# Float16 pairs for the scores of every second group of four heads, and six weight groups converted beside the attention

## The chip, the cores and the metric

One core of a Trainium2 chip. The time is the device time of one execution in microseconds. Engines: TensorE (PE, with its weight loads as PEld), VectorE (DVE), ScalarE (ACT), GpSimd (POOL) and SyncE (SP), whose queue issues nearly all transfers.

## The reference

Sigmoid attention, then a gated layer on its output, with q, k and v in float32 and the weights in float64:

```python
scores = scale * np.matmul(q, k.transpose(0, 1, 3, 2)) - np.log(S)   # 8 batches, 12 heads, S = 448, head size 64
attn = 1.0 / (1.0 + np.exp(-scores))
attn_out = np.matmul(attn, v)
x = attn_out.transpose(0, 2, 1, 3).reshape(B * S, H * D)             # 3584 x 768
gate = 1.0 / (1.0 + np.exp(-(x @ w_gate)))                           # w_gate, w_val: 768 x 1536
val = x @ w_val
out = gate * val @ w_out                                             # w_out: 1536 x 768
```

## The kernel before

It runs in two stages. The first is the attention, with the conversion of some weights beside it; the second the gated layer, in visits: four pairs of batches, each visited for two parts of the hidden size ("A"), then the output ("C"). Its products are in float16 pairs: a float32 value is scaled by a power of two and split into a high half (a cast) and a low half (value times scale minus the high half), and three products (high by high, high by low, low by high) go into one accumulator. They are formed by seven products in place of eight (N_OPS = 7 operands per block).

**The attention.** A group m is four heads of one batch, two pairs p of two heads h; there are 24. `load_qk` and `load_v` bring q, k and v of a group. A beat (m, g), g from 0 to 6, is one call of `scores` and, LAG = 2 beats behind it, one of `values`. `scores` fills a PSUM tile `sc` by four float32 products of 64x64 array tiles (L502; each is two instructions in the trace), so that four run side by side, and ScalarE makes `a` of it with one sigmoid over 896 columns (L510). `values` multiplies by v into accumulators `av` (L527). Two accumulators per pair hold the two halves of the keys; `finish` copies one by ScalarE (L537), and VectorE adds the other (L544). The result goes to DRAM and is read back as x.

Two PSUM tiles `sc` exist, and three `a`; every engine works through its instructions in the order written.

**The weights** come as 64-bit floats. `Words` loads a block of 128x384 (a chunk; `AHEAD` of them are loaded ahead) and turns it into float32 by integer operations: the magnitude of the upper words (L214) by VectorE, a limit by GpSimd (L195), then in `first` two VectorE instructions (L201, L202), in `second` three (L209 to L211), and a maximum (L107). `convert` does this in steps, two to a chunk: an even step holds `first` and the next chunk's magnitude, an odd one the limit and `second`. Eight steps make a group (one of the twelve halves of jp, `halves_of_jps`). Six steps later its scale is known: the largest value of each row, clamped (L116), is spread over the partitions by TensorE (`told`, L508, which writes beside the scores in `sc`) and ScalarE (L513), and VectorE makes powers of two of it (L126, L120 to L123). Then seven operands are cast by GpSimd (L377, with sums by L259 for four of them), two steps later VectorE makes the low halves (L229), and SP stores them. In the step the low halves come first, then the maximum, then the chunk's own work, then what falls due of a scale.

FIRST groups are converted in the attention, the others of part 0 in the first visit, all others later. `BESIDE` says how many steps are done by which beat (`done`, in the loop over beats). After the steps, the beat does the work on x of the first pair: loads with maxima, sums, and splits (L385 is the low half) from certain m on.

**The order of a beat** is scores, values, loads, stores, weight steps, adds, x. In the visits a tick is one product group of nine instructions (L659); `beside` runs the weight steps due at each tick, and `Visit.tick` the loads, sums and splits of the next x. `load_operands` keeps RING + BEYOND = 11 operands loaded or known ahead.

Of the kernel before, what the change touches and what calls it, by code (L numbers as in the profile page):

```python
# [20 lines left out]
P = 128  # L21
# [9 lines left out]
BESIDE = 146, 168  # L31

AHEAD, AHEAD_FF = 4, 3

FIRST = 7
# [20 lines left out]
def sigmoid_attention_glu_kernel(ctx: ExitStack, tc: tile.TileContext, qk, v, wg, wv, wo, out):  # L56
# [111 lines left out]
    class Words:  # L168
# [28 lines left out]
        def first(self):  # L197

            raw, f = self.begun[0]
            e = f.bitcast(U32)  # L200
            nc.vector.tensor_scalar(out=e, in0=e, scalar1=3, scalar2=0x3F800000, op0=ALU.logical_shift_left, op1=ALU.bitwise_and)  # L201
            nc.vector.scalar_tensor_tensor(out=e, in0=raw[:, :, 1], scalar=0xC0000000, in1=e, op0=ALU.bitwise_and, op1=ALU.bitwise_or)  # L202

        def second(self):

            raw, f = self.begun.pop(0)
            self.spent += 1
            m = self.pool.tile([P, CW], U32, tag="wm", name="wm", bufs=1)
            nc.vector.tensor_scalar(out=m, in0=raw[:, :, 1], scalar1=11, scalar2=0x80000000, op0=ALU.logical_shift_left, op1=ALU.bitwise_or)  # L209
            nc.vector.scalar_tensor_tensor(out=m, in0=raw[:, :, 0], scalar=21, in1=m, op0=ALU.logical_shift_right, op1=ALU.bitwise_or)  # L210
            nc.vector.scalar_tensor_tensor(out=f, in0=m, scalar=2.0 ** -31, in1=f, op0=ALU.mult, op1=ALU.mult)  # L211
# [266 lines left out]
    with tc.manual_schedule(), tc.tile_pool(name="att", bufs=2) as att, tc.tile_pool(name="sc", bufs=2, space=PSUM) as scp, \  # L478
            tc.tile_pool(name="av", bufs=1, space=PSUM) as avp:
        loads, avs, pending, adds, stores = {}, {}, [], [], []  # L480

        def load_qk(m):

            if m < B * NQ:
                loads[m] = [att.tile([P, 2, 2 * S], F32, tag="qk", name="qk")]
                nc.sync.dma_start(out=loads[m][0], in_=qk[m // NQ, m % NQ])

        def load_v(m):
            if m < B * NQ:
                loads[m].append(att.tile([P, 7, 2, D], F32, tag="v", name="v"))  # L490
                nc.sync.dma_start(out=loads[m][1], in_=v[m // NQ, m % NQ])

        def scores(m, g):


            qkt = loads[m][0]
            sc = scp.tile([P, 2, 512], F32, tag="sc", name="sc")
            for h in range(2):
                for u in range(2):
                    p = u if g == 3 else g // 4  # L500
                    k0 = S + (3 * P if g == 3 else g % 4 * P + u * HP)
                    nc.tensor.matmul(sc[halves[u], h, :S], lhsT=qkt[halves[h], p, k0:k0 + HP], rhs=qkt[halves[h], p, :S],  # L502
                                     start=True, stop=True)
            told = spreads[:1]
            for sp in told:
                spreads.remove(sp)
                for h in range(2):
                    nc.tensor.matmul(sc[:, h, S:], lhsT=sp.each, rhs=ident[:, halves[h]], start=True, stop=True)  # L508
            a = att.tile([P, 2, S], F32, tag="a", name="a", bufs=3)
            nc.scalar.activation(a, sc[:, :, :S], AF.Sigmoid, bias=bias, scale=scale)  # L510
# [5 lines left out]
        def values(m, g, a):  # L516

            vt = loads[m][1]
            for u in range(2):
                p = u if g == 3 else g // 4  # L520
                key = (2 * m + p, u)
                start = key not in avs
                if start:
                    avs[key] = avp.tile([P, 512], F32, tag=f"av{p}{u}", name="av")
                last = (3 if u == 0 else 2) if p == 0 else 6
                for h in range(2):
                    nc.tensor.matmul(avs[key][halves[h], :S], lhsT=vt[halves[u], g, h], rhs=a[halves[u], h],  # L527
                                     start=start, stop=g == last)
            if g == 3:
                finish(2 * m)  # L530
            if g == 6:
                finish(2 * m + 1)

        def finish(n):
            b, c = divmod(n, 2 * NQ)
            x = att.tile([P, S], F32, tag="x", name="x", bufs=3)
            nc.scalar.copy(x, avs.pop((n, 0))[:, :S])  # L537
            adds.append((beat, x, avs.pop((n, 1))[:, :S]))
            stores.append((beat + 3, b, c, x))

        def finish_adds(wait=0):
            while adds and adds[0][0] + wait < beat + (not wait):
                _, x, other = adds.pop(0)
                nc.vector.tensor_tensor(out=x, in0=other, in1=x, op=ALU.add)  # L544
# [38 lines left out]
        beat = 0  # L583
        for m in range(B * NQ):
            for g in range(7):
                pending.append((m, g, scores(m, g)))
                if len(pending) > LAG:
                    values(*pending.pop(0))
                if g == 0:
                    load_qk(m + 1)  # L590
# [4 lines left out]
                while done < n_chunks and done * BESIDE[0] < beat * n_chunks or \  # L595
# [469 lines left out]
```

## Time and profile before

| | |
|---|---|
| median of 3 runs (lowest, highest) | 1126.88 us (1126.84, 1127.08) |
| the profiled execution's own time | 1127.14 us |
| its span | 1125.4 us |
| TensorE, VectorE, ScalarE, GpSimd busy | 99%, 70%, 60%, 44% |
| attention | up to 261.98 us |
| granted clock of TensorE | 0.999 |

A row of the timeline is: start in us, length in us, engine, line, operation, tile written and read, count, and in brackets the idle time before it and what ended it. A row of groups has count, busy us, mean ns, and idle time. Mean times of TensorE's products are pipelined, and four tiles overlap: 537 ns is not what one costs.

### The profile page before, as it was taken

What the parts mean: (1) busy time and instruction counts of PE and PEld (TensorE: products, weight loads), DVE (VectorE), ACT (ScalarE), POOL (GpSimd) and SP (SyncE); (2) the same over time, 40 slices, a digit from 0 to 9 for tenths busy, and PEclk for the clock granted to TensorE, in tenths of its full rate; (3) what the DMA queues carried; (4) which work ended last, traced back from release to release, by engine and by line L of the source; (5) the groups of instructions that cost most, each with busy time, mean ns of one, the idle gap of its engine ahead of it and who ended that gap; (6) DMA issues with size and microseconds to landing.
All of it is one profiled execution on the core that took longest, in us unless ns stands there. A gap on an engine that the chain in (4) does not pass through costs nothing.

```text
span 1125.4 us, 20712 instructions
## 1 busy us (share of the span) xinstructions
PE 1119.5 (99%) x7269; PEld 554.4 (49%) x7269; DVE 790.4 (70%) x1318; ACT 672.2 (60%) x1265; POOL 496.9 (44%) x424
## 2 busy tenths in 40 slices
PE   9999999999999999999999999999999999999998
PEld 4444434445555555555555555555555555555554
DVE  3578989974574555667678887887348687676863
ACT  6777778876775765766565756666444444253430
POOL 0045778791252332253233443333365294572940
PEclk9999999999999999999999999999999999999999
DMA  7679979888687746753566798979756876867644
GB/s 254 233 245 326 320 251 316 302 281 303 241 274 254 254 144 213 265 163 104 151 216 207 236 355 256 322 235 256 223 167 200 252 225 206 277 199 247 190 127 140
DMA packets 174536, 265.30 MB, mean 236 GB/s; under 512 B 49248, under 2 KB 151392, under 8 KB 174432
## 3 DMA queue, kind: packets, MB, share of 16 engines
q1 hardware_dynamic: 174144, 263.80, 72.6%
q8 instruction: 57, 0.93, 0.3%
q14 instruction: 47, 0.39, 0.1%
q10 hardware_dynamic: 288, 0.18, 0.1%
HBM read 182.48 MB, written 81.43 MB: 235 GB/s over the span
## 4 chain that ended last, share of the span: by engine, by line
PE 99%; ACT 0%; DVE 0%; DVEq 0%; issue 0%
PE un L659 76%; PE av L527 11%; PE sc L502 11%; PE sc L565 0%; PE sc L508 0%; ACT a L510 0%; PE un L627 0%; DVE g L944 0%; DVEq L1060 0%; DVE bias L79 0%; DVEq L944 0%
## 5 line engine op out<-in xcount | busy, mean ns | idle before, releaser
L659 PEld LDWEIGHTS <-A 128*128 128x128 f16 x3024 | 295.5, 98 | 275.8 <-issue 0.7
L659 PE MATMUL un<-b,A 128*128 128x448 f16 x1512 | 296.6, 352 | 0.0
L659 PE MATMUL un<-b,v 128*128 128x448 f16 x1512 | 296.3, 352 | 0.0
L659 PE MATMUL un<-hh,A 128*128 128x448 f16 x1008 | 273.0, 352 | 0.0
L659 PEld LDWEIGHTS <-v 128*128 128x128 f16 x1512 | 147.8, 98 | 137.7
L510 ACT ACTIVATE a<-sc,bias 128x896 f32<-128x896 f32 x168 | 169.5, 1010 | 62.4 <-PE sc L502 54.5
L659 PE MATMUL un<-hl,A 128*128 128x448 f16 x504 | 177.6, 352 | 0.0
L527 PE MATMUL av<-a,v 64*64 64x448 f32 x1344 | 166.5, 537 | 0.0
L502 PE MATMUL sc<-qk 64*64 64x448 f32 x1344 | 165.8, 537 | 0.4 <-ACT a L510 0.4
L869 POOL TENSOR_TENSOR g<-c,g 128x448 f32<-128x448 f32 x44 | 59.1, 1344 | 184.9 <-DVE c L642 98.2
L195 POOL TENSOR_SCALAR wf<-wf 128x384 f32<-128x384 f32 x72 | 41.9, 582 | 204.3 <-ACT wf L217 131.8
L854 ACT ACTIVATE g<-c,back 128x448 f32<-128x448 f32 x72 | 48.2, 670 | 77.6 <-DVE c L642 75.1
L502 PEld LDWEIGHTS sc<-qk 64*64 64x64 f32 x1344 | 56.1, 133 | 74.7 <-issue 59.5
L642 DVE TENSOR_TENSOR c<-un,u 128x448 f32<-128x448 f32 x72 | 44.8, 622 | 66.6 <-PE un L659 58.3
L527 PEld LDWEIGHTS av<-a,v 64*64 64x64 f32 x1344 | 56.0, 133 | 68.9 <-issue 64.8
L259 POOL TENSOR_TENSOR wf<-wf 128x384 f32<-128x384 f32 x72 | 82.7, 1154 | 13.2 <-DVE whl L229 12.2
L345 POOL TENSOR_TENSOR v<-v 128x448 f32<-128x448 f32 x48 | 64.0, 1362 | 51.6 <-DVE hl L385 50.6
L345 POOL TENSOR_TENSOR b<-b 128x448 f32<-128x448 f32 x48 | 67.5, 1442 | 40.6 <-DVE hl L385 40.6
L675 ACT COPY p<-un 128x448 f32<-128x448 f32 x48 | 25.6, 533 | 57.9 <-PE un L659 57.6
L345 POOL TENSOR_TENSOR r<-r 128x448 f32<-128x448 f32 x36 | 46.5, 1306 | 24.2 <-DVE b L385 23.8
L544 DVE TENSOR_TENSOR x<-av,x 128x448 f32<-128x448 f32 x48 | 29.8, 620 | 38.8 <-ACT x L537 37.6
L104 ACT ACTIVATE junk<-g 128x448 bf16<-128x448 f32 x88 | 50.7, 576 | 7.4 <-POOL g L869 5.9
(348 smaller groups left out, 1361.2 us busy)
## 6 DMA issues: line engine op xcount, KB each, us to landing
A<-ad SPq DMA_DIRECT2D x168, 192.0 KB, 3.3
A<-oo SPq DMA_DIRECT2D x168, 192.0 KB, 2.6
qk<-qk SPq DMA_DIRECT2D x23, 896.0 KB, 5.5
h<-g SPq DMA_DIRECT2D x88, 224.0 KB, 3.4
ad<-whl SPq DMA_DIRECT2D x84, 192.0 KB, 4.1
bd<-b SPq DMA_DIRECT2D x30, 448.0 KB, 3.5
b<-bd SPq DMA_DIRECT2D x30, 448.0 KB, 5.8
v<-vv SPq DMA_DIRECT2D x24, 448.0 KB, 5.1
```

The lines of the kernel that those rows point to most:

```text
L104: nc.scalar.activation(junk[:, :x.shape[-1]], x, AF.Abs, accum_out=to)
L195: nc.gpsimd.tensor_scalar(out=f, in0=f, scalar1=F32_MAX, scalar2=F64_ZERO, op0=ALU.min, op1=ALU.max)
L259: nc.gpsimd.tensor_tensor(out=x, in0=y, in1=z, op=op)
L345: engine.tensor_tensor(out=to, in0=x, in1=y, op=ALU.subtract)
L502: nc.tensor.matmul(sc[halves[u], h, :S], lhsT=qkt[halves[h], p, k0:k0 + HP], rhs=qkt[halves[h], p, :S], start=True, stop=True)
L510: nc.scalar.activation(a, sc[:, :, :S], AF.Sigmoid, bias=bias, scale=scale)
L527: nc.tensor.matmul(avs[key][halves[h], :S], lhsT=vt[halves[u], g, h], rhs=a[halves[u], h], start=start, stop=g == last)
L544: nc.vector.tensor_tensor(out=x, in0=other, in1=x, op=ALU.add)
L642: engine.tensor_tensor(out=to, in0=x, in1=y, op=ALU.add)
L659: nc.tensor.matmul(acc, lhsT=w, rhs=m, start=begin and i == 0, stop=i == len(terms) - 1, skip_group_check=not begin)
L854: nc.scalar.activation(gates[i], acc, AF.Sigmoid, scale=of_unit[0])
L869: nc.gpsimd.tensor_tensor(out=h, in0=acc, in1=gates[i], op=ALU.mult)
```

## The change

- Groups with odd m (`in_halves`) have their scores in float16 pairs: `split_qk` makes, beside group m - 1, the largest magnitudes of q and k (one reduction), their clamped values `told`, and, from the sums `total` over the partitions (TensorE products with `ones`, a ScalarE copy), powers of two; then high and low halves `hl` of q and k, 896 columns at a time. `scores` then does three rounds of four products, in the order (low k, high q), (high k, low q), (high k, high q). The sigmoid's scale becomes `back`. Even groups stay in float32.
- `scores` and `values` pair the array tiles by p in place of key halves, so each pair has one accumulator (two tiles in PSUM each) and the add is gone; a copy is made per beat, and stored two beats later, not three.
- A scale's spread is done by 64x64 tiles, four to a scale, in place of two 128x128 products.
- q and k of a group are loaded two groups ahead, in three tiles; the first group's loads are cut differently, and group 1's stand ahead of the first v.
- `second` is one instruction: the lower word's top three bits are put in, in place of the product of a rounded mantissa; `first` keeps 30 bits.
- FIRST is 6, not 7: the first visit converts two groups. `PACE` replaces `BESIDE`: 58% of the 50 chunk steps by beat 77, all by 150, then the rest. `AHEAD` is 3, not 4. The work on x starts as before at m = 7 (loads), with five loads a group, sums from m = 9, splits from m = 11, two a group; in the first visit the splits start at tick 33.

```diff
-BESIDE = 146, 168
-AHEAD, AHEAD_FF = 4, 3
-FIRST = 7
+PACE = (0, 0), (77, 0.58), (150, 1)
+AHEAD, AHEAD_FF = 3, 3
+FIRST = 6
...
         def second(self):
-            m = self.pool.tile([P, CW], U32, tag="wm", name="wm", bufs=1)
-            nc.vector.tensor_scalar(out=m, in0=raw[:, :, 1], scalar1=11, scalar2=0x80000000, op0=ALU.logical_shift_left, op1=ALU.bitwise_or)
-            nc.vector.scalar_tensor_tensor(out=m, in0=raw[:, :, 0], scalar=21, in1=m, op0=ALU.logical_shift_right, op1=ALU.bitwise_or)
-            nc.vector.scalar_tensor_tensor(out=f, in0=m, scalar=2.0 ** -31, in1=f, op0=ALU.mult, op1=ALU.mult)
+            e = f.bitcast(U32)
+            nc.vector.scalar_tensor_tensor(out=e, in0=raw[:, :, 0], scalar=29, in1=e, op0=ALU.logical_shift_right, op1=ALU.bitwise_or)
...
+        def split_qk(m):
+            if m >= B * NQ or not in_halves(m):
+                return
+            x = loads[m]
...
+            nc.vector.tensor_reduce(out=each, in_=x.rearrange("r p t s -> r t p s"), axis=AX.XY, op=ALU.max,
+                                    apply_absolute_value=True)
+            nc.vector.tensor_scalar(out=told, in0=each, scalar1=SUM_MAX, scalar2=TINY, op0=ALU.min, op1=ALU.max)
+            yield
+            total = att.tile([P, 2, 2], F32, tag="qka", name="qka", bufs=1)
+            qk_sums.append((told, total))
+            yield
+            yield
...
+            nc.vector.tensor_tensor(out=m_, in0=total[:, 0], in1=total[:, 1], op=ALU.add)
+            powers(m_, s_, inv)
+            nc.vector.tensor_scalar(out=back, in0=inv[:, 0:1], scalar1=inv[:, 1:2], scalar2=scale, op0=ALU.mult, op1=ALU.mult)
+            hl = att.tile([P, 2, 2, 2, S], F16, tag="hl", name="hl", bufs=1)
+            parts[m] = hl, back
+            for t in range(2):
+                nc.vector.tensor_scalar(out=hl[:, 0, t], in0=x[:, :, t], scalar1=s_[:, t:t + 1], scalar2=None, op0=ALU.mult)
+            yield
+            for t in range(2):
+                nc.vector.scalar_tensor_tensor(out=hl[:, 1, t], in0=x[:, :, t], scalar=s_[:, t:t + 1], in1=hl[:, 0, t],
+                                               op0=ALU.mult, op1=ALU.subtract)
+                yield
...
+            for i, (kt, qt) in enumerate(((1, 0), (0, 1), (0, 0)) if in_halves(m) else ((None, None),)):
+                for h in range(2):
+                    for p in range(2):
+                        qs, ks_ = (x[halves[h], qt, 0, p], x[halves[h], kt, 1, p, ks]) if in_halves(m) else \
+                            (x[halves[h], p, 0], x[halves[h], p, 1, ks])
+                        nc.tensor.matmul(sc[halves[p], h, :S], lhsT=ks_, rhs=qs, start=i == 0, stop=i == 2 or not in_halves(m))
+            sums = qk_sums[:1]
...
+                        nc.tensor.matmul(sc[halves[u], h, S:S + 2], lhsT=ones[halves[h]], rhs=sp[halves[h]], start=True, stop=True)
...
-            adds.append((beat, x, avs.pop((n, 1))[:, :S]))
-            stores.append((beat + 3, b, c, x))
+                stores.append((beat + 2, b, c, x))
...
                 if g == 0:
-                    load_qk(m + 1)
+                    load_qk(m + 2)
+                if (m, g) == (0, 1) or m > 0 and g == 0:
+                    splitting = split_qk(m + 1)
+                next(splitting, None)
...
-                while done < n_chunks and done * BESIDE[0] < beat * n_chunks or \
-                        n_chunks <= done < n_weights and (done - n_chunks) * (BESIDE[1] - BESIDE[0]) < (beat - BESIDE[0]) * (n_weights - n_chunks):
+                while done < due_at(beat) - 1e-6:
                     next(weights)
                     done += 1
-                finish_adds(1)
...
-                if m >= first_x and g in (1, 3, 5):
+                if m >= first_x and g not in (0, 4):
                     next(x_loads, None)
-                if m >= first_x + 4 and g in (2, 6):
+                if m >= first_x + 2 and g in (2, 6):
                     next(x_sums, None)
-                if m >= first_x + 7 and (g in (2, 5) or g == 0 and m % 2):
+                if m >= first_x + 4 and g in (2, 5):
                     next(splits, None)
...
-            if p >= 29:
+            if p >= (29 if self.v_ else 33):
                 next(self.splits, None)
...
-    for ticks, n in ((range(2, 34), n_first), (calm[:-last], n_chunks), (calm[-last:], last)):
+    for ticks, n in ((range(2, 33), n_first), (calm[:-last], n_chunks), (calm[-last:], last)):
```

More of the change, by code (lines that the diff above doesn't have):

```diff
@@ L29 @@
 BF16_MAX = 3.3895313892515355e38
[L31 to L35 removed]
+PACE = (0, 0), (77, 0.58), (150, 1)
+AHEAD, AHEAD_FF = 3, 3
+SUM_MAX = 2.0 ** 119
+FIRST = 6
 LAG = 2
@@ L507, in scores @@
                 for h in range(2):
-                    nc.tensor.matmul(sc[:, h, S:], lhsT=sp.each, rhs=ident[:, halves[h]], start=True, stop=True)
+                    for u in range(2):
+                        nc.tensor.matmul(sc[halves[u], h, S:], lhsT=sp.each[halves[h], halves[u]], rhs=ident[halves[h], halves[h]],
+                                         start=True, stop=True)
             a = att.tile([P, 2, S], F32, tag="a", name="a", bufs=3)
-            nc.scalar.activation(a, sc[:, :, :S], AF.Sigmoid, bias=bias, scale=scale)
+            nc.scalar.activation(a, sc[:, :, :S], AF.Sigmoid, bias=bias, scale=unit)
+            for _, total in sums:
+                nc.scalar.copy(total, sc[:, :, S:S + 2])
             for sp in told:
@@ L516, in values, with finish_copy @@
         def values(m, g, a):
[L518 to L525, printed above, removed]
+            vt = values_of[m]
+            if g == 0:
+                avs[m] = [avp.tile([P, 512], F32, tag=f"av{p}", name="av") for p in range(2)]
+            for p in range(2):
                 for h in range(2):
[L527 to L530, printed above, removed]
+                    nc.tensor.matmul(avs[m][p][halves[h], :S], lhsT=vt[halves[p], g, h], rhs=a[halves[p], h],
+                                     start=g == 0, stop=g == 6)
             if g == 6:
[L532 to L537, printed above, removed]
-            adds.append((beat, x, avs.pop((n, 1))[:, :S]))
-            stores.append((beat + 3, b, c, x))
[L541 to L544, printed above, removed]
+                copies.extend((2 * m + p, acc) for p, acc in enumerate(avs.pop(m)))
+        def finish_copy():
+            if copies:
+                n, acc = copies.pop(0)
+                b, c = divmod(n, 2 * NQ)
+                x = att.tile([P, S], F32, tag="x", name="x", bufs=3)
+                nc.scalar.copy(x, acc[:, :S])
+                stores.append((beat + 2, b, c, x))
         def finish_stores():
@@ L609, in sigmoid_attention_glu_kernel @@
             values(*pending.pop(0))
-            finish_adds()
-        beat += 3
+        while copies:
+            finish_copy()
+        beat += 2
         finish_stores()
```

63 lines of the change are left out of this document (39 added, 24 removed).

## The prediction

> **What bounds the kernel now.** I read the page's engine shares and its chain first, then the chain in order of time, the windows, and the attention's instructions in the timeline.
>
> ```profile
> PE 1119.5 (99%) x7269; PEld 554.4 (49%) x7269; DVE 790.4 (70%) x1318; ACT 672.2 (60%) x1265; POOL 496.9 (44%) x424
> PE un L659 76%; PE av L527 11%; PE sc L502 11%; PE sc L565 0%; PE sc L508 0%; ACT a L510 0%; PE un L627 0%; DVE g L944 0%; DVEq L1060 0%; DVE bias L79 0%; DVEq L944 0%
> ```
> ```profile
> 16.43 0.75 PE sc L502 x8
> ...
> 43.49 0.75 PE sc L502 x8
> ...
> 261.98 34.16 PE un L659 x180
> ```
> ```profile
> 140.00:180.00 40.00, 40.00 (x428) 16.08 (x424) 36.46 (x71) 31.61 (x40) 33.42 (x29) 1.00 0.82 266
> 180.00:220.00 40.00, 40.00 (x432) 15.98 (x427) 39.08 (x77) 31.75 (x40) 29.74 (x24) 1.00 0.91 304
> 280.00:300.00 20.00, 20.00 (x108) 10.33 (x106) 11.35 (x21) 15.43 (x44) 6.39 (x7) 1.00 0.90 315
> ```
>
> TensorE sets the end everywhere; nothing else in the chain has a whole per cent. In the attention (to 261.98) one beat is a group of score products and one of value products: 18 beats from 16.43 to 43.49 make 1.503 us each, 0.752 a half. A float16 pass of 448 columns takes 34.16/180 = 0.190 us in the visits. In the windows (columns PE, PEld, DVE, ACT, POOL) TensorE is full while VectorE is at 91 and 98% of 140 to 220: it is busy with weights and nobody on TensorE waits for it. The change lets TensorE wait for it.
>
> **TensorE, what is removed.** An odd group m makes each score group of three float16 rounds, each of four 64x64 tiles, in place of four float32 products. No row shows 64x64 float16 tiles. Bounds: the four tiles side by side, as the float32 ones run, give 3 x 0.190 = 0.569 us; no gain would leave 0.752, rival 3 is worse. I take 0.569, since issue is no limit. From the timeline:
>
> ```profile
> 3.93 0.27 PEld L502 LDWEIGHTS sc<-qk 64*64 64x64 f32 x8 [1.17 <-issue]
> ...
> 37.27 0.96 PE L502 MATMUL sc<-qk 64*64 64x448 f32 x8
> ...
> 38.35 1.01 ACT L510 ACTIVATE a<-sc,bias 128x896 f32<-128x896 f32 x1 [0.49 <-PE sc L502]
> ...
> 140.50 0.93 PE L502 MATMUL sc<-qk 64*64 64x448 f32 x8
> ...
> 141.37 0.23 PE L508 MATMUL sc<-ident,each 128*128 128x64 bf16 x2
> ...
> 141.70 1.01 ACT L510 ACTIVATE a<-sc,bias 128x896 f32<-128x896 f32 x1 [0.20 <-PE sc L508]
> ...
> 142.33 0.93 PE L502 MATMUL sc<-qk 64*64 64x448 f32 x8
> 142.60 0.26 ACT L513 COPY all<-sc 128x128 f32<-128x128 f32 x1
> ```
>
> Eight loads went out within 0.27 us after a wait, 0.034 each, and twelve per 0.569 need 0.047. Gain: 84 odd beats x (0.752 - 0.569) = 15.4 us. A beat with a scale's spread (128x128 among 64x64) takes 142.33 - 140.50 = 1.83 us, 0.33 more than 1.503; eight of these become seven in 64x64 tiles, and twelve `ones` groups come in. Between 0 and 0.23 each (the L508 row); I take 0.08: 8 x 0.33 - 19 x 0.08 = 1.1 us gained. Together 16.5.
>
> **VectorE, what is removed and added.** Gone are the 48 adds (L544), two of the three instructions of `second`, and one weight group. None is on the path: nothing of TensorE waits for them. Added for every odd m: a reduction, `told`, six small ones, two `hi`, two `lo`. Groups up to 262 us, then the timeline:
>
> ```profile
> L544 DVE TENSOR_TENSOR x<-av,x 128x448 f32<-128x448 f32 x47 | 29.1, 620 | 36.5 <-ACT x L537 35.3 <-PE sc L502 1.0
> L209 DVE TENSOR_SCALAR wm<-wraw 128x384 uint32<-128x384 uint32 x28 | 16.3, 582 | 0.0
> L211 DVE SCALAR_TENSOR_TENSOR wf<-wm,wf 128x384 f32<-128x384 uint32 x28 | 17.1, 610 | 1.0
> L107 DVE TENSOR_REDUCE x0c<-g 128x1 f32<-128x448 f32 x4 | 2.4, 610 | 0.0
> L107 DVE TENSOR_REDUCE w10c<-wf 128x1 f32<-128x384 f32 x4 | 2.2, 547 | 0.0
> L116 DVE TENSOR_SCALAR each<-w00m 128x128 bf16<-128x128 f32 x1 | 0.2, 227 | 0.0
> ```
> ```profile
> 15.00 0.56 DVE L210 SCALAR_TENSOR_TENSOR wm<-wraw,wm 128x384 uint32<-128x384 uint32 x1
> ...
> 19.77 0.35 DVE L214 TENSOR_SCALAR wf<-wraw 128x384 uint32<-128x384 uint32 x1
> ...
> 225.33 0.68 DVE L385 SCALAR_TENSOR_TENSOR b<-xt,x0s,b 128x448 f16<-128x448 f32 x1
> 225.92 0.61 DVE L229 SCALAR_TENSOR_TENSOR whl<-wf,w21s,whl 128x384 f16<-128x384 f32 x1
> ...
> 241.62 0.15 DVE L120 TENSOR_SCALAR invw<-w30m 128x1 uint32<-128x1 uint32 x1
> 241.81 0.15 DVE L121 TENSOR_SCALAR w30s<-invw 128x1 uint32<-128x1 uint32 x1
> 242.00 0.15 DVE L122 TENSOR_SCALAR w30s<-w30s 128x1 f32<-128x1 f32 x1
> 242.07 0.14 DVE L123 TENSOR_SCALAR invw<-invw 128x1 f32<-128x1 f32 x1
> ```
>
> Undisturbed: `hi` (896 elements), from 0.227 at 128 and 0.35 at 384, is 0.60; `lo`, from 0.61 at 384 and 0.68 at 448, 1.15; the reduction (1792), from 547 and 610 ns, 1.95; a small one starts 0.19 after one it needs, 0.07 after another (starts overlap: L122 to L123). Six small ones make 0.9.
>
> **The new wait.** An odd m's scores start with the low half of k, the last thing `split_qk` makes (`lo` with t = 1, in beat 5 of the even m before). What is behind it: `total` comes from TensorE's `ones` and a ScalarE copy in beat 2. Let T be the start of scores(m, 0), m even. Beat 2 starts at T + 3.01; its activation starts 38.35 - 37.27 = 1.08 later, 0.08 more for the `ones`, runs 1.01, and the copy ends some 0.1 after it (the L513 copy ends 0.15 after): `total` is there at T + 5.28. scores(m+1, 0) is due at T + 7 x 1.503 = T + 10.52, so VectorE has 5.14 us (0.1 for the hand-over). In this time stand the small ones 0.9, `hi` 1.05 and `lo` 2.2 (less overlaps) = 4.15, and, in program order, every weight step of beats 3 and 4. While TensorE waits there, values(m, 5) and all scores behind it wait too, and so does ScalarE.
>
> Which steps these are follows from `PACE`: step 32, for one, falls into beat 3 of m = 12, the first beat where due_at exceeds 32. From beat 77 a step comes every 73/21 = 3.48 beats, four in 14, so each pair of groups finds the same kind in the same place: for even m from 10 to 20 a split, a maximum, the next magnitude and `first` (0.61 + 0.55 + 0.35 + 0.35 + 0.56 less overlaps = 2.2 us; none of the magnitude at 20), at 12, 16 and 20 the finish of a scale too, 0.85. Earlier, the beats hold the end of a conversion or a maximum of x (m = 2, 6, 8: about 0.5 us, which fits), and at m = 4 all but the split (1.6).
>
> Waits of TensorE, undisturbed: m+1 = 11, 15, 19: 4.15 + 2.2 - 5.14 = 1.2 each; 13, 17: 2.05; 21: 1.75; 23 (two splits): 0.1; 5: 0.6. m = 1 starts its split one beat late, with 3.64 us to spare and 1.35 of steps: 1.85. Sum 12.0.
>
> VectorE is disturbed beside GpSimd, which the windows show at 74 to 84%. Groups from 140 to 220 us:
>
> ```profile
> L229 DVE SCALAR_TENSOR_TENSOR whl<-wf,w20s,whl 128x384 f16<-128x384 f32 x6 | 5.8, 960 | 0.0
> L229 DVE SCALAR_TENSOR_TENSOR whl<-wf,w11s,whl 128x384 f16<-128x384 f32 x7 | 5.3, 760 | 0.0
> L209 DVE TENSOR_SCALAR wm<-wraw 128x384 uint32<-128x384 uint32 x10 | 5.2, 520 | 0.0
> L385 DVE SCALAR_TENSOR_TENSOR b<-xt,x0s,b 128x448 f16<-128x448 f32 x4 | 3.4, 859 | 0.0
> ```
>
> These took 520 ns against 0.35 (one source), 859 against 0.68 and 760 to 960 against 0.61 (two). In proportion to size, `hi` x 1.5, `lo` x 1.25 and 0.4 for the step are 1.6 us per late segment; as a fixed delay of 0.17 per large instruction, 1.1. I take 1.3 x 7 = 9.1, and 0.6 for m = 5 to 9; the ends are 0 and 1.6 x 7 + 1 = 12.2. The Trainium skill, "SBUF — State Buffer", section "Who interferes with whom", has the two engines take a shared port pair as an exclusive lock, so that the loser waits for the end of the other's instruction. By that rule the delay would not grow with the tile, 1.1 would hold, and the sum would be 1.4 us lower; L107's 547 and 610 ns, of an operation that it exempts, agree.
>
> **The rest.** Start: a first weight magnitude that waits for its load stands ahead of the first reduction.
>
> ```profile
> 6.74 0.33 PEld L527 LDWEIGHTS av<-a,v 64*64 64x64 f32 x8 [0.42 <-DMA v<-vv]
> ...
> 9.49 0.36 DVE L214 TENSOR_SCALAR wf<-wraw 128x384 uint32<-128x384 uint32 x1 [8.41 <-DMA wraw<-wg]
> ```
>
> With qk(1) and all of qk(0) ahead of v on the queues (896 KB more), v lands near 8.7 instead of 6.74; today TensorE loses 6.8 us in all before it runs evenly (261.98 less 168 x 1.503 less the spreads). With the first `told` near 12.2 I count +0.5, between -1 and +2. The stores of x go out a beat earlier on SP with no add to wait for; the load of qk one group earlier; neither ends a wait in this attention, 0. The first visit converts two groups, 34 steps in 31 ticks of 9 x 0.190 us: hidden by TensorE's own work (20.00 of 20.00 in 280 to 300, ScalarE 15.43, VectorE 11.35). The first group's operands are stored by tick 26 and used from 39, 22 us later; if that cover were gone, each tick late would cost 1.7. Splits from tick 33 end with the visit. 0.
>
> **Sum**, against this execution's 1127.14 (span 1125.4, 1.7 around it): -16.5 + 12.0 + 9.7 + 0.5 = +5.7, 1132.8; the median of the runs lies 0.26 lower, so 1132.6. Ends: no disturbance, 1122; full, and the bad start, 1137.
>
> **Rivals.**
>
> 1. The split hides. If the weight steps of beats 3 and 4 don't decide (VectorE meets the 5.14 us), only m = 1 and the start cost: -16.5 + 2.4, 1113. For it: 4.15 alone fits, and VectorE has some 4 us idle ahead of `total`. Against it: program order. It decides as soon as the late segments need less than 5.14 us; break-even with before is at an average wait of 1.9 us per late segment.
>
> 2. `hi` at one element per cycle of its float32 source, 0.35 at 384 becoming twice the slope: +0.45 each in some ten segments, 1142. Against it: L116 (float32 to bfloat16, 227 ns) lies on the line of L214.
>
> 3. Loads of 64x64 float16 tiles don't hide behind the products. Four float32 loads take 0.18 us together in a round, under the products before them; exposed in each of three rounds, a half beat is 3 x 0.37 = 1.11 us, 30 us more than now over 84 beats, and the waits stay: 1178.
>
> ```profile
> 36.15 0.18 PEld L527 LDWEIGHTS av<-a,v 64*64 64x64 f32 x4 [0.20 <-issue]
> ```
> The Trainium skill, "TensorEngine Tiling (Array Packing)", section "Restrictions", says that column tiling disables the fast weight load; no run here shows such a load in float16.
>
> 4. The clock falls in waits of 3 us and more.
>
> ```profile
> L502 PE MATMUL sc<-qk 64*64 64x448 f32 x1344 | 165.8, 537 | 0.4 <-ACT a L510 0.4
> L565 PE MATMUL sc<-bias 64*64 64x448 f32 x16 | 3.2, 962 | 1.0 <-DVE bias L79 1.0
> ```
>
> The first 16 products took 962 ns against 537 later, so an idle TensorE starts slow. Three late waits come near 3.3 us; 1.7 us more behind each, 1137.5. The Trainium skill, "TensorE: Matmul & The Clock Gate", section "HAM oscillation — how this bites in real kernels", warns of gaps above about 3.4 us; in the quoted windows the granted clock is 1.00, and TensorE has no such gap there to show it.
>
> **How the numbers follow.** The forecast has 0.48, rival 1 0.32, rival 2 0.10, rivals 3 and 4 0.05 each. Within 0.2% (2.3 us, about what a measurement of this kernel can tell from no change) lies 0.07 of the forecast's chance, faster 0.06, slower 0.35. Slower: 0.35 + 0.20 = 0.55; same 0.07; faster 0.32 + 0.06 = 0.38. The forecast's own range is 1122 to 1137; to leave out no more than 2 in 10, 1111 to 1142.
>
> **What would show it.** Scores of odd groups at 0.57 us a group; TensorE's longest waits at the first load of odd m, on the second `lo`, 2 to 4 us from m = 11 on, near 1.8 at m = 1 and none at 3; VectorE idle ahead of its add of `total`; visits unchanged from the first product on. If odd scores start on time, rival 1 holds; if their rounds take over 0.3 us, rival 3; if `hi` takes 1 us with GpSimd idle, rival 2; if the clock drops behind a wait, rival 4.

## The result, and the profile after

The changed kernel takes 1143.02 us (median of 4 runs, 1140.20 to 1145.58) where the kernel before took 1126.91 beside it: a ratio of 1.0143, 95% interval 1.0127 to 1.0152. The forecast was slower by 5.7 us; it is slower by 16.1, which is 6 us beyond the end of the forecast's own range (1137) and 1 us beyond that of the wider one (1142). The profiled execution took 1143.63 us, with a span of 1141.9, 16.5 more than before.

From the page of the changed kernel: engine shares, the chain by engine and by line, and the two groups of score products.

```profile
PE 1109.8 (97%) x7666; PEld 550.8 (48%) x7666; DVE 760.1 (67%) x1263; ACT 683.8 (60%) x1296; POOL 491.8 (43%) x417
...
PE 87%; DVE 7%; DMA 3%; ACT 1%; issue 1%; SPq 0%; POOL 0%; DVEq 0%; ACTq 0%
PE un L710 72%; PE av L569 8%; PE sc L539 7%; DVE hl L518 2%; DVE hl L515 1%; DVE wf L204 1%; DMA wraw<-wg 1%; DMA r<-xd 1%; DMA g<-xd 1%; ACT a L554 1%; DVE whl L229 1%; DMA v<-ad 1%; DVE wf L203 0%; DVE qkm L499 0%; DMA xd<-x 0%
...
L539 PE MATMUL sc<-qk 64*64 64x448 f32 x672 | 80.1, 550 | 0.8 <-DMA qk<-qk 0.5
L539 PE MATMUL sc<-hl 64*64 64x448 f16 x1008 | 63.1, 353 | 15.3 <-DVE hl L518 15.3
```

VectorE is busy for less time than before (760 against 790 us) and yet has 7% of the chain, where it had nothing: it now stands ahead of TensorE. Line numbers have moved: scores L539, `ones` L545, values L569, reduction L499, `told` L501, `hi` L515, `lo` L518, products of the visits L710. The waits of the attention (0 to 300 us; total, times, longest):

```profile
DVE qk L509 <- ACT qka L556: 29.4, 9, 4.8
PEld L539 <- DVE hl L518: 23.0, 12, 3.8
...
PE sc L545 <- DVE qkt L501: 6.3, 2, 4.9
...
PE av L569 <- DMA v<-vv: 2.8, 1, 2.8
```

The first and second are the forecast's: VectorE idle ahead of `total`, and TensorE waiting for `lo`. The third, TensorE waiting for `told`, is not in it; the last, for v, is in it only as 0.5 of the start.

Where the 16.5 us come from, by the starts of scores(m, 0) in both timelines: the first scores start 0.7 later (4.71 against 4.01) and group 0 takes 17.3 us where it took 10.7, so group 1 starts 7.3 later than before; the beat of the `ones` of m = 10 is 5.9 longer than 1.50, and slow products behind it add 0.8; the first scores of odd m from 5 on are 16.9 late together; slow products behind the wait of m = 15 add 1.7; the attention ends at 276.74 against 261.92, 14.8 later. That leaves 17.8 for the gain. The visits add 1.8, all by the 270th product. The beats give nearly the same gain: 84 x 0.183 = 15.4 by float16, less 12 x 0.06 for the `ones`, and 3.2 that e1_f32 below, without float16, gains from m = 1 to the attention's end.

### The profile page after: what moved, and what is told of

It is laid out like the page before. It is cut to its first block, busy times and chain, and to the rows that moved or that the text cites. A ratio compares the mean times of both kernels' runs of the same rounds, so it can differ in the third digit from the quotient of the medians.

```text
span 1141.9 us, 21412 instructions
## 1 busy us (share of the span) xinstructions
PE 1109.8 (97%) x7666; PEld 550.8 (48%) x7666; DVE 760.1 (67%) x1263; ACT 683.8 (60%) x1296; POOL 491.8 (43%) x417
## 4 chain that ended last, share of the span: by engine, by line
PE 87%; DVE 7%; DMA 3%; ACT 1%; issue 1%; SPq 0%; POOL 0%; DVEq 0%; ACTq 0%
PE un L710 72%; PE av L569 8%; PE sc L539 7%; DVE hl L518 2%; DVE hl L515 1%; DVE wf L204 1%; DMA wraw<-wg 1%; DMA r<-xd 1%; DMA g<-xd 1%; ACT a L554 1%; DVE whl L229 1%; DMA v<-ad 1%; DVE wf L203 0%; DVE qkm L499 0%; DMA xd<-x 0%
## 5 line engine op out<-in xcount | busy, mean ns | idle before, releaser
L710 PEld LDWEIGHTS <-A 128*128 128x128 f16 x3024 | 295.0, 98 | 276.9 <-DMA xd<-x 0.9
L710 PE MATMUL un<-b,A 128*128 128x448 f16 x1512 | 296.8, 353 | 0.4 <-ACT x L579 0.4
L710 PE MATMUL un<-b,v 128*128 128x448 f16 x1512 | 296.5, 353 | 0.0
L710 PE MATMUL un<-hh,A 128*128 128x448 f16 x1008 | 273.1, 353 | 0.0
L710 PEld LDWEIGHTS <-v 128*128 128x128 f16 x1512 | 147.5, 98 | 137.7
L710 PE MATMUL un<-hl,A 128*128 128x448 f16 x504 | 177.7, 353 | 0.0
L569 PE MATMUL av<-a,v 64*64 64x448 f32 x1344 | 159.4, 549 | 2.8 <-DMA v<-vv 2.8
L554 ACT ACTIVATE a<-sc,bias 128x896 f32<-128x896 f32 x84 | 84.5, 1007 | 43.8 <-PE sc L539 30.5
L554 ACT ACTIVATE a<-sc,bias,qkb 128x896 f32<-128x896 f32 x84 | 92.6, 1102 | 28.7 <-PE sc L539 18.5
L539 PE MATMUL sc<-qk 64*64 64x448 f32 x672 | 80.1, 550 | 0.8 <-DMA qk<-qk 0.5
L539 PE MATMUL sc<-hl 64*64 64x448 f16 x1008 | 63.1, 353 | 15.3 <-DVE hl L518 15.3
L569 PEld LDWEIGHTS av<-a,v 64*64 64x64 f32 x1344 | 48.5, 136 | 47.9 <-issue 34.2
L539 PEld LDWEIGHTS <-hl 64*64 64x64 f16 x1008 | 29.6, 108 | 65.4 <-issue 35.7
L693 DVE TENSOR_TENSOR c<-un,p 128x448 f32<-128x448 f32 x48 | 29.9, 623 | 46.8 <-PE un L710 45.3
```

Of the source, the lines that this page charges most:

```text
L539: nc.tensor.matmul(sc[halves[p], h, :S], lhsT=ks_, rhs=qs, start=i == 0, stop=i == 2 or not in_halves(m))
L569: nc.tensor.matmul(avs[m][p][halves[h], :S], lhsT=vt[halves[p], g, h], rhs=a[halves[p], h], start=g == 0, stop=g == 6)
L693: engine.tensor_tensor(out=to, in0=x, in1=y, op=ALU.add)
L710: nc.tensor.matmul(acc, lhsT=w, rhs=m, start=begin and i == 0, stop=i == len(terms) - 1, skip_group_check=not begin)
```

## The experiments

A lead is the start of some work against its start in the kernel before, in the profiled executions, in us (negative is earlier). The last column is the 271st product of the first visit. The times are medians, the leads belong to one execution each: that of e9_m4_whole is the fastest of its ten (1125.16), those of e13_m4_fixed and e14_act are the slowest of theirs (1128.66 and 1127.82).

| run | time, ratio [95% interval] | m = 1 | m = 11 | m = 16 | m = 22 | m = 23 | attention's end | in the visit |
|---|---|---|---|---|---|---|---|---|
| changed kernel | 1143.02, 1.0143 [1.0127, 1.0152] | 7.3 | 10.4 | 12.3 | 13.7 | 17.0 | 14.8 | 16.6 |
| e1_f32 | 1128.55, 1.0015 [1.0005, 1.0024] | 2.2 | 1.4 | 0.8 | -0.1 | 0.0 | -0.9 | 0.4 |
| e10_f32_v | 1126.44, 0.9992 [0.9983, 1.0002] | 0.6 | -0.2 | -0.8 | -1.7 | -1.6 | -2.6 | -1.4 |
| e4_m1 | 1139.14, 1.0114 [1.0099, 1.0129] | 4.4 | 7.6 | 7.8 | 8.9 | 12.2 | 10.0 | 12.3 |
| e8_m4 | 1133.26, 1.0059 [1.0042, 1.0076] | 2.0 | 4.5 | 5.6 | 4.7 | 6.4 | 4.2 | 5.9 |
| e9_m4_whole | 1127.96, 1.0009 [0.9999, 1.0018] | 3.1 | 3.1 | 0.1 | -2.1 | -1.4 | -3.6 | -2.0 |
| e2_whole | 1140.64, 1.0123 [1.0108, 1.0138] | 6.7 | 8.3 | 8.8 | 8.2 | 12.6 | 11.8 | 14.1 |
| e3_xslow | 1143.77, 1.0151 [1.0135, 1.0166] | 6.1 | 2.6 | 2.9 | 4.7 | 10.9 | 10.1 | 15.2 |
| e13_m4_fixed | 1127.18, 0.9997 [0.9988, 1.0006] | 1.8 | -1.3 | -4.2 | -6.3 | -3.6 | -4.1 | 1.2 |
| e7_combo | 1131.79, 1.0045 [1.0030, 1.0060] | 0.2 | -4.9 | -8.9 | -7.0 | 0.7 | 0.7 | 3.5 |
| e14_act | 1124.34, 0.9979 [0.9969, 0.9988] | 1.3 | -2.9 | -6.8 | -9.2 | -4.9 | -5.4 | -0.7 |
| e17_after_act | 1140.93, 1.0133 [1.0111, 1.0154] | 5.8 | 7.5 | 11.3 | 12.1 | 14.1 | 11.9 | 14.7 |
| e11_early | 1120.16, 0.9937 [0.9922, 0.9952] | 1.7 | -4.1 | -7.1 | -8.0 | -8.0 | -8.8 | -7.7 |
| e12_early_first7 | 1125.52, 0.9985 [0.9975, 0.9995] | 1.8 | -1.8 | 0.8 | 0.0 | 0.0 | -0.9 | 0.1 |
| e15_act_to21 | 1120.19, 0.9941 [0.9926, 0.9956] | 0.5 | -4.5 | -8.3 | -10.7 | -10.7 | -11.6 | -7.8 |
| e16_early_act | 1118.54, 0.9925 [0.9908, 0.9941] | 1.4 | -4.3 | -7.3 | -8.3 | -8.2 | -9.1 | -8.5 |

Two theories for the late scores ran through them. The order: VectorE has the time, but weight steps stand between `hi` and `lo` in its row. The load: VectorE and GpSimd have too much to do beside float16 groups, wherever `lo` stands.

**What is not float16.** `e1_f32` keeps every group in float32, `e10_f32_v` loads v ahead of qk(1) as well, `e4_m1` makes only group 1 float32.

```diff
-            return m % 2 == 1
+            return False                     # e1_f32 and e10_f32_v
+            return m % 2 == 1 and m > 1      # e4_m1
...
-            load_qk(1)                       # e10_f32_v: the same call behind load_v(0)
```

> All groups of heads keep float32 scores; the rest of the change stays (pairing by p, no adds, spreads in 64x64 tiles, one-instruction end of the conversion, six weight groups, the new pace, the new loads at the start). Theory A (the loss is waiting for the split of q and k): no wait for halves and none for told at m = 0 and 10; 84 x 0.183 = 15.4 us of TensorE come back, 16.9 of waits at the first scores of odd groups, 6.7 at m = 10, 1.7 of slow clock at m = 15 and most of the 5 at the start go. 1131 us, +-2, with v late at the start (2.8) and the first visit's 1.8 still there. Rival B (the other parts, weights and visits, cost as much): 1136 or more.

> All groups in float32, and v of group 0 ahead of q and k of group 1. Theory D (896 KB ahead of v delay the first values): the 1.1 to 2 us that group 0 lost against before go, 1126.7 us, +-0.7. Rival: the transfers share the engines, so the order matters little, 1128.5.

> Group 1 keeps float32 scores, so no split runs beside group 0; all else as changed (v of group 0 is still behind q and k of group 1). Theory A (the start loses by the wait for told and by the half clock that follows the two waits): told's 1.4 us and 2 to 3 us of slow clock go, 1.3 of TensorE's gain in group 1 goes too: 1140 us, +-1.5. Rival D (the start is set by v's landing alone): 1144.

Without float16 the rest of the change costs nothing that can be told in the attention (2.2 lost by m = 1, 0.9 ahead at its end) and 1.3 in the visit; the time is 0.5 us below the range of theory A, and rival B is out. Timelines of TensorE, e1_f32 and then e10_f32_v:

```profile
7.32 0.98 PE L539 MATMUL sc<-qk 64*64 64x448 f32 x8 [0.36 <-ACT a L554]
10.10 0.98 PE L569 MATMUL av<-a,v 64*64 64x448 f32 x8 [1.79 <-DMA v<-vv]
```
```profile
8.55 0.93 PE L569 MATMUL av<-a,v 64*64 64x448 f32 x8
```

With v first its wait is gone, 1.6 us at m = 1 and 2.1 in the time. Float32 in group 1 saves 2.9 at m = 1, and theory A's time for it came. So the changed kernel's start (7.3) is v, then the split of group 1 behind it. The size of each part is loose, since runs that are alike up to m = 1 scatter there: 5.8 to 7.3 with both faults (the changed kernel, e3, e17), 2.0 to 4.4 with float32 in group 1 (e1, e4, e8, e9), 0.2 to 1.8 with v first as well (e7, e10, e11, e13 to e16). In e4_m1, which waits 2.5 us for v, the products behind start 1.4 to 1.5 us apart until 13.5, in place of 0.75; in e1_f32 (1.8) and e8_m4 (1.5) they do not, so the slow pace can follow the wait for v alone. In the visit, e10_f32_v still has this wait, at the spread of the second weight group's scale:

```profile
PEld L678 <- DVE each L118: 1.5, 1, 1.5
```

**The order.** `e8_m4` has float16 in m = 3, 7, 11, 15, 19, 23 alone; `e9_m4_whole` the same, with the low halves right behind the high ones; `e2_whole` does that to the changed kernel.

```diff
-            return m % 2 == 1
+            return m % 4 == 3                # e8_m4 and e9_m4_whole
...
-            yield                            # e9_m4_whole and e2_whole: both yields
             for t in range(2):
                 nc.vector.scalar_tensor_tensor(out=hl[:, 1, t], ...
-                yield
```

> Float16 pairs for every fourth group alone (m = 3, 7, 11, 15, 19, 23), six splits and not twelve; the order within the beats as changed. Six groups save 7.7 us of TensorE against all float32 (1128.5). Theory A (the weight steps written between total and the second low half decide): the waits at 11, 15, 19 and 23 stay as they were, 1.2 + 2.4 + 2.2 + 3.2: 1130 us, +-1.5. Theory C (the load decides): with half of the splits they go: 1121.5, +-1.5.

> As the run with every fourth group, and the low halves right behind the high ones. Theory A: the four late waits go, 1121.5 us, 8 less than with the weight steps between. Theory C: 1121.5 too, and no difference between the two. A wait for told (C in part) would show at m = 10, 14, 18 or 22.

> The two low halves are written right behind the high ones, in the same beat, so no weight step stands between them in VectorE's order; nothing else is changed. Theory A (program order in the 5.14 us between total and the due scores decides): the waits at m = 5, 9 and 11 to 23, 16.9 us together, fall to 3 or less; m = 10's wait for told and the start stay: 1130 us, +-3. Rival C (VectorE's load decides, the order only places the wait): the waits turn up at told of the next even groups, and the time stays within 3 us of 1143.

Waits of the attention, e8_m4 and then e9_m4_whole:

```profile
PEld L539 <- DVE hl L518: 10.6, 6, 3.1
```
```profile
PE sc L543 <- DVE qkt L501: 3.1, 1, 3.1
...
PEld L537 <- DVE hl L517: 1.4, 2, 1.1
```

Two deleted yields take 5.3 us: with a float16 group in every fourth place, order is nearly the whole of the wait for `lo` (1.4 of 10.6 us stays). The times of both runs missed their expectations, e8_m4 by 1.8 beyond theory A's range and e9_m4_whole by 6.5: theory A did not count the 3.1 us at `told` of m = 10, which both have, and the rest of e9_m4_whole's miss is open. In the changed kernel the same edit takes 2.4 us, as rival C has it. The waits for `lo` at m = 5, 11, 13, 15, 17 and 21 go there too, that of m = 23 grows from 3.2 to 4.4, and waits for `told` come in at beat 2 of m = 8, 14, 18 and 20 beside those of m = 0 and 10 (e2_whole: 12.7 us, 6 times). VectorE and then TensorE of e2_whole at m = 14:

```profile
159.74 1.00 DVE L385 SCALAR_TENSOR_TENSOR b<-g,x0s,b 128x448 f16<-128x448 f32 x1 [2.41 <-POOL b L377]
...
162.90 2.01 DVE L499 TENSOR_REDUCE qkm<-qk 128x2 f32<-128x1792 f32 x1
165.01 0.25 DVE L501 TENSOR_SCALAR qkt<-qkm 128x2 bf16<-128x2 f32 x1
```
```profile
165.32 0.22 PE L543 MATMUL sc<-qkt,ones 64*64 64x2 bf16 x4 [3.01 <-DVE qkt L501]
```

VectorE stood 2.41 us behind a cast of x by GpSimd, with the reduction of the next group behind it in its row. Fixing the order moves the wait to the next thing that VectorE delivers late.

**The work on x.** `e3_xslow` gives the changed kernel the x pace of before; `e13_m4_fixed` is e9_m4_whole, and `e7_combo` all odd groups from 3 on, each with that pace, v first and low halves behind high ones. `e14_act` is e7_combo with the casts of the x split all on ScalarE, `e17_after_act` the changed kernel with that alone.

```diff
-                if m >= first_x and g not in (0, 4):
+                if m >= first_x and g in (1, 3, 5):
                     next(x_loads, None)
-                if m >= first_x + 2 and g in (2, 6):
+                if m >= first_x + 4 and g in (2, 6):
                     next(x_sums, None)
-                if m >= first_x + 4 and g in (2, 5):
+                if m >= first_x + 7 and (g in (2, 5) or g == 0 and m % 2):
                     next(splits, None)
...
-        splits = split_x(0, scaled_in_turn)
+        splits = split_x(0, scaled)          # e14_act and e17_after_act
```

> Loads, sums and splits of x go back to the pace of the kernel before (three loads a group, sums from m = 11, splits from m = 14, 2.5 a group); all else as changed. Theory A (at m = 10 VectorE was late for told because maxima of x, five a group, waited for their loads and filled it): the 5.9 us at told and the 0.8 of slow clock behind it go, the late waits grow by up to 0.4 each with the denser splits: 1137 us, +-2. Rival C (VectorE has no room at all in the middle): the wait turns up at another even group, 1143 +-2.

> float16 pairs in groups 3, 7, 11, 15, 19 and 23, low halves right behind the high ones, v ahead of the second q and k, x at the pace of before. The run without the last two edits took 1127.96, with 3.3 us at the ones of group 10 and about 2.2 us at the start of group 1. If these two are the x loads in VectorE's row and the place of v, both go: 1122 to 1123.5. If the waits are those of float16 groups as such, 1127 to 1129 again.

> Four edits at once: the low halves right behind the high ones, x at the pace of before, v of group 0 ahead of q and k of group 1, and group 1 in float32. Theory A (order in VectorE's queue): each edit takes away its own wait, 12 to 14 us at the late groups, 6.7 at m = 10, 5 at the start: 1120 us, +-3. Theory C (from group 8 on VectorE and GpSimd have no room beside eleven splits; order moves a wait, as in the two runs before): the start's 4 and some 2 to 3 more, 1136 us, +-3.

> The run with float16 pairs in all odd groups from 3 on, low halves behind the high ones, v first and x at the pace of before (1131.79), with all casts of the x split on ScalarE, none on GpSimd. There VectorE stood 8.8 us behind GpSimd's casts between 130 and 262 us, and about 15 us were lost in groups 16 to 23. If GpSimd's cast is what makes VectorE late, the low halves of x (L385) no longer wait for POOL, the losses in groups 16 to 23 fall under 6 us, and the time is 1120 to 1125. If VectorE simply has too much to do there, the time is 1130 to 1133 again. If ScalarE becomes the late one (its sigmoids and copies behind the casts), waits for ACT appear on TensorE and the time is above 1133.

> The changed kernel (1143.02) with nothing but the casts of the x split on ScalarE. If GpSimd's casts are a cause of its own in the changed order too, the first scores of groups 13 to 23 wait less and 2 to 6 us go: 1137 to 1141. If there the low halves are late by their place in VectorE's row alone, the time is 1142 to 1144. The wait at the ones of group 10 (4.9 us, behind x loads, ahead of any split's cast) stays in both.

In e3_xslow the wait at m = 10 is gone: between m = 8 and 11 it loses 0.9 us where the changed kernel loses 7.5. It is all given back later, 6.2 at the end of group 22 and 5.1 in the visit, so that the time is rival C's. e13_m4_fixed missed its expectation in the same places: 6.3 us ahead at m = 22, it lost 2.7 there and 5.3 into the visit. Slower x leaves more work on x for the end; that this pile alone makes the loss is not shown.

e7_combo lies between its two theories, 8.8 above theory A's range for the sum of the single waits: it was 8.9 ahead at m = 16 and behind before at m = 23; e14_act kept its lead up to m = 22. Waits from 120 to 262 us, e7_combo and then e14_act:

```profile
DVE b L385 <- POOL b L377: 8.8, 4, 2.8
PE sc L543 <- DVE qkt L501: 6.6, 4, 3.0
PEld L537 <- DVE hl L517: 6.1, 2, 5.5
```
```profile
PEld L537 <- DVE hl L517: 5.4, 2, 4.8
DVE whl L229 <- POOL whl L377: 5.3, 7, 1.1
...
PE sc L543 <- DVE qkt L501: 0.8, 2, 0.6
```

Moving those casts takes 7.4 us: VectorE was held by GpSimd, not full. What stays is 4.3 us ahead of m = 23. VectorE adds `total` there 9.3 us after scores(22, 0), where 5.28 was forecast for every group; 1.4 us of its time before that are waits for GpSimd's casts of weights (L229), the rest is work in its own row. In the changed kernel the same move takes 2.1, with ranges that overlap (1139.94 to 1145.66 against 1140.20 to 1145.58); in the traces the late scores of m = 13 to 23 go from 13.5 to 11.5. So in the changed kernel either edit alone, the order or the casts, is worth some 2 us; which of the two is the larger part there is not shown.

**Fewer float16 groups.** `e11_early` is e7_combo with float16 only in m = 3 to 13, `e16_early_act` adds the move of the casts, `e12_early_first7` a seventh weight group, `e15_act_to21` is e14_act without group 23.

```diff
-            return m % 2 == 1
+            return m % 2 == 1 and 1 < m < 14     # e15_act_to21: 1 < m < 22
...
-FIRST = 6
+FIRST = 7                                        # e12_early_first7 alone
```

> float16 pairs only in the odd groups 3 to 13, the low halves right behind the high ones, v loaded ahead of the second q and k, the x work at the pace of the kernel before. The run of the same with float16 pairs up to group 23 stood 8.87 us ahead of the kernel before at the start of group 16 and lost all of it, and more, in groups 16 to 23. Theory (each float16 group pays about 1.4 us on TensorE while VectorE and GpSimd have room beside it, and the loss is theirs): nothing is lost behind group 14, so the attention ends 8 to 10.6 us early, the first visit gives 1.3 to 1.9 back, and the time is 1117 to 1121. Rival (the x work compressed into fewer groups alone makes VectorE late, float16 or not): waits of 2 us and more at the ones products of groups 16 to 22 again, and 1127 to 1132.

> The run beside it (float16 pairs in the odd groups 3 to 13), with seven weight groups beside the attention in place of six. If the wait in the first visit is for VectorE behind its second weight group, it goes with that group: 1.3 to 1.9 us less than the run beside it. If the seventh group's own scan and split beside the attention meets VectorE where it is full, a wait of 1 to 3 us appears at the ones products or the first scores of a group, and the two times are the same or this one the longer.

> float16 pairs in the odd groups 3 to 21, low halves behind the high ones, v first, x at the pace of before, casts of the x split on ScalarE. The run with group 23 too took 1124.34 and lost 4.2 us at the end of group 22. If that loss belongs to the last float16 group, whose scores are the last work before the visits and find VectorE behind the last weight splits, it goes with it: attention end 8 to 10 us ahead of before, 1118 to 1121, no better than 1120.16 by more than 2. If the loss is the weight split's own, it stays: 1123 to 1125.

> Control: the best version so far (float16 pairs in groups 3 to 13, 1120.16) with the casts of the x split on ScalarE. No late wait is left there from group 14 on, so if the gain of 7.4 us from this move in the run with all odd groups came from VectorE's waits for GpSimd, nothing is gained here: 1119.5 to 1121. If the move is a gain of its own: 1116 or less.

e11_early beats before by 6.9 us, e16_early_act by 8.5: six float16 groups, each ahead of the splits of x, and no late wait. From the page of e16_early_act:

```profile
PE 1110.4 (99%) x7474; PEld 580.0 (52%) x7474; DVE 720.4 (64%) x1191; ACT 686.3 (61%) x1300; POOL 470.6 (42%) x407
...
PE 96%; DVE 1%; DMA 1%; issue 1%; POOL 0%; ACT 0%; SPq 0%; DVEq 0%; POOLq 0%
```

VectorE is down to 1% of the chain. The control expected no gain; 1.6 us came, of which its lead shows 0.3 at the attention's end and 0.9 in the visit, so the move's 7.4 us in e14_act are mostly the waits. e12 confirms that the wait in the visit belongs to its second weight group (none of it left), though its visit still loses 1.0 us, all by the 90th product, where e11_early loses 1.2; but between m = 8 and 14 it is 8 us behind e11_early, in waits at beat 2 and at the first scores of 13: the seventh group's price, and the other side of its expectation. e15_act_to21 has no loss at m = 22 and the best lead, 11.6, and gives 3.8 back in the visit, 2.7 of it as it begins, where TensorE's wait of 2.6 is put down to the last copies of x by ScalarE (L577). The attention has become early enough for what the visit needs to be late.

## Why the prediction was right or wrong

| step | forecast | measured |
|---|---|---|
| TensorE's gain | 16.5 | 17.8, by difference |
| start, with m = 1 | 2.35 | 7.3 |
| late scores, m = 5 to 23 | 19.85 | 16.9 |
| `told` at m = 10 | 0 | 6.7 (5.9 and 0.8 of slow products) |
| slow products behind m = 15 | 0 (rival 4) | 1.7 |
| first visit | 0 | 1.8 |

The measured column, the gain taken off, adds up to 16.6. Two steps failed that the prediction took as given: that `total` is there at the same time in every group, and that the start costs little. They make 11.7 of the 10.9 us by which it fell short; the other rows nearly cancel.

**Right: the gain.** An odd beat takes 1.32 us, the forecast's 0.569 + 0.752; a beat with a spread 1.56 where it was 1.83, one with `ones` 1.56 in place of 1.50 (0.06, forecast 0.08).

**Right: the split's wait.** VectorE and then TensorE at m = 14:

```profile
167.66 0.16 DVE L509 TENSOR_TENSOR qk<-qka 128x2 f32<-128x2 f32 x1 [1.02 <-ACT qka L556]
...
168.67 1.27 DVE L515 TENSOR_SCALAR hl<-qk,qk 128x896 f16<-128x896 f32 x2
169.86 0.61 DVE L229 SCALAR_TENSOR_TENSOR whl<-wf,w10s,whl 128x384 f16<-128x384 f32 x1
170.39 0.55 DVE L109 TENSOR_REDUCE w20c<-wf 128x1 f32<-128x384 f32 x1
...
172.17 3.27 DVE L518 SCALAR_TENSOR_TENSOR hl<-qk,qk,hl 128x896 f16<-128x896 f32 x2
```
```profile
175.50 0.88 PE L539 MATMUL sc<-hl 64*64 64x448 f16 x12 [2.27 <-DVE hl L518]
176.16 1.72 PE L569 MATMUL av<-a,v 64*64 64x448 f32 x8
177.65 1.34 PE L539 MATMUL sc<-hl 64*64 64x448 f16 x12
...
179.85 0.74 PE L539 MATMUL sc<-hl 64*64 64x448 f16 x12
```

Scores(14, 0) start at 162.47, so `total` was forecast for 167.75 and came at 167.66; the weight steps between `hi` and `lo` are the ones named, and scores(15, 0) come 2.44 late, forecast 1.2 + 1.3. For m = 11 to 23 the forecast had 18.65 and 14.7 came. The disturbance term (1.3 in each of the seven) was mis-sized and in the wrong places: m = 13, 17 and 21 are late by 2.0, 2.0 and 1.7, which is the undisturbed forecast (2.05, 2.05, 1.75), and m = 23 by 3.2 where 0.1 + 1.3 was forecast, for the reason given below. `hi` was put at 0.60 x 1.5 = 0.90 and took 0.68. That the sum came near is in part luck, since errors of both signs are in it. Groups of 140 to 235 us, where GpSimd is busy 63% (59.52 of 95):

```profile
L518 DVE SCALAR_TENSOR_TENSOR hl<-qk,qk,hl 128x896 f16<-128x896 f32 x8 | 9.9, 1277 | 0.0
...
L515 DVE TENSOR_SCALAR hl<-qk,qk 128x896 f16<-128x896 f32 x8 | 5.1, 680 | 0.0
```

**Wrong: "+0.5, between -1 and +2" for the start, and 1.85 for m = 1.** TensorE and then VectorE of group 0:

```profile
10.96 0.98 PE L569 MATMUL av<-a,v 64*64 64x448 f32 x8 [2.84 <-DMA v<-vv]
...
14.46 0.22 PE L545 MATMUL sc<-qkt,ones 64*64 64x2 bf16 x4 [1.36 <-DVE qkt L501]
14.49 1.79 PE L569 MATMUL av<-a,v 64*64 64x448 f32 x8
```
```profile
11.92 0.36 DVE L214 TENSOR_SCALAR wf<-wraw 128x384 uint32<-128x384 uint32 x1 [10.77 <-DMA wraw<-wg]
12.20 2.01 DVE L499 TENSOR_REDUCE qkm<-qk 128x2 f32<-128x1792 f32 x1
14.24 0.17 DVE L501 TENSOR_SCALAR qkt<-qkm 128x2 bf16<-128x2 f32 x1
...
18.08 1.15 DVE L518 SCALAR_TENSOR_TENSOR hl<-qk,qk,hl 128x896 f16<-128x896 f32 x1
```

v landed 2.3 us after the 8.7 estimated, the magnitude waited to 11.92 where before had 9.49, and `told` came at 14.41, not 12.2, so `ones` made TensorE wait a second time. The products behind start 1.5 us apart up to 19.0, where 0.75 is their pace: TensorE, interrupted twice, ran at half speed (granted clock 0.84 over the first 22 us, 1.00 before the change). The estimate priced each load alone and not TensorE's speed between them. The split of m = 1 itself was then in time: its wait is 0, since group 0 had stretched.

**Wrong: "`total` is there at T + 5.28", used for every even m.** It takes `told` to be ready by beat 2 and VectorE to stand idle ahead of `total`. At m = 2, 4, 6, 12, 16 and 18 it has 3.0 to 4.8 us idle there, at m = 14 and 20 only 1.0 and 0.9, at m = 8, 10 and 22 none. `total` is then added 6.7, 10.8 and 7.2 us after scores(m, 0):

```profile
98.32 0.14 DVE L509 TENSOR_TENSOR qk<-qka 128x2 f32<-128x2 f32 x1
...
259.25 0.15 DVE L509 TENSOR_TENSOR qk<-qka 128x2 f32<-128x2 f32 x1
```

So the scores of m = 9 are 1.35 late (undisturbed forecast: 0), and of the 3.2 at m = 23 some 1.9 were lost ahead of `total`, where VectorE stood behind low halves of weights and of x and waited 1.4 for GpSimd's casts. The worst is m = 10. VectorE and then TensorE:

```profile
112.77 0.62 DVE L109 TENSOR_REDUCE x0c<-g 128x1 f32<-128x448 f32 x1 [0.68 <-DMA g<-xd]
114.57 0.62 DVE L109 TENSOR_REDUCE x0c<-g 128x1 f32<-128x448 f32 x1 [1.18 <-DMA g<-xd]
...
119.04 2.00 DVE L499 TENSOR_REDUCE qkm<-qk 128x2 f32<-128x1792 f32 x1
121.15 0.51 DVE L501 TENSOR_SCALAR qkt<-qkm 128x2 bf16<-128x2 f32 x1
```
```profile
121.71 0.22 PE L545 MATMUL sc<-qkt,ones 64*64 64x2 bf16 x4 [4.90 <-DVE qkt L501]
```

Scores(10, 0) start at 112.88; the reduction, written in beat 0, begins 6.2 us later, behind maxima of x that wait 1.9 us for their loads and behind weight work. The five x loads a group of the diff are in no term of the prediction; their maxima stand on VectorE's row, ahead of `told`. e3_xslow, with three a group and the sums begun later, has no such wait at m = 10 and none at m = 9.

**Wrong: first visit "0".** Hidden work has an end that TensorE meets: the spread of the second group's scale, 1.2 us by product 225 (e12 shows the cause), and about 0.6 at the visit's start, whose cause is open.

**The rivals.** 1 did not hold as written; with the low halves moved and half the float16 groups (e9_m4_whole) the split nearly hides, with 1.4 us of waits for `lo`. 2 is out (`hi` 0.68, expected near 1), 3 is out (beats of 1.32, loads hidden). 4 held in part, in group 0 and at m = 10 and 15, and not by its condition, waits of 3 us and more; its time (1137.5) is 1137.7 by its own terms, 1132.6 and three times 1.7.

## What to carry to other kernels

Work that one engine makes for another is ready only when everything written ahead of it in that engine's row is done, with all that this waits for: an engine at 67% of the span set the end here because what TensorE needed next stood in its row behind other work, and that work behind another engine's casts and loads. Idle time that is there for one group is not there for every group: read it at each. When such a wait is removed, ask what is delivered late next; with eleven splits it was `told`, then the visit's operands, and the best kernel put fewer splits where the row had room. A trade of TensorE time for VectorE time is worth taking per place, not for all groups at once.

## What the runs showed of the hardware that was not expected

TensorE went to half speed after a wait shorter than rival 4's 3 us, and not after each longer one. At m = 15, after 2.27 us of idle time, a round of twelve took 1.34 us in place of 0.74 (rows above), and the granted clock of that window (the column before the last two) is 0.91:

```profile
160.00:180.00 20.00, 17.73 (x202) 7.14 (x196) 18.27 (x31) 13.56 (x17) 15.81 (x14) 0.91 0.78 265
```

At m = 23 of the same execution, after 3.01 us, the rounds kept their pace (in e8_m4 the rounds of m = 11 kept theirs after 2.35 us, and those of m = 15 fell to 1.33 after 2.27):

```profile
265.87 0.76 PE L539 MATMUL sc<-hl 64*64 64x448 f16 x12 [3.01 <-DVE hl L518]
...
267.21 0.74 PE L539 MATMUL sc<-hl 64*64 64x448 f16 x12
```

The Trainium skill, "TensorE: Matmul & The Clock Gate", section "What's actually happening", has a free-running window of about 3.4 us; that the length of a wait alone does not decide agrees with it, though no row shows that its place in time does, while a fall after 2.27 us does not agree with its rule of a whole idle window of that length.

VectorE is delayed beside GpSimd in single instructions, not in all of them. By their times in the trace, `lo` (two sources) took 1.14 or 1.15 us in 21 of 24 cases, eight of them with GpSimd at work beside it; the other three, all with GpSimd at work beside them, took 1.96, 1.89 and 1.46 (m = 10 and 14). `hi` (one source) took 0.68 us in 22 of 24 cases, and GpSimd did nothing beside any of these, so its mean in the table above shows no immunity; the two beside GpSimd's casts, at m = 22, took 0.84 and 0.91. At m = 18 two instructions of two elements took 0.58 and 0.53 us beside GpSimd, in place of 0.16 and 0.17, so the delay does not grow with the tile. Rows of m = 18 and m = 22:

```profile
213.54 0.58 DVE L509 TENSOR_TENSOR qk<-qka 128x2 f32<-128x2 f32 x1 [3.00 <-ACT qka L556]
214.15 0.53 DVE L122 TENSOR_SCALAR qk<-qk 128x2 uint32<-128x2 uint32 x1
...
258.78 4.64 POOL L377 TENSOR_SCALAR whl<-wf,w21s 128x384 f16<-128x384 f32 x3 [0.60 <-DVE w21s L124]
...
260.65 1.67 DVE L515 TENSOR_SCALAR hl<-qk,qk 128x896 f16<-128x896 f32 x2
```

The Trainium skill, "SBUF — State Buffer", section "Who interferes with whom", has only instructions of VectorE with two sources or in its two-port modes contend with GpSimd; the rows agree only if `hi` and the small one of L122, with one source each, are in such a mode, which no row shows. The prediction's reading of that section, a delay that does not grow with the tile, agrees with the two rows of m = 18.
